# An attention-plus-dense kernel rebuilt: masks as a product, head pairs in one array, the dense stage between attention steps, the max as a relu

## The chip, the cores and the metric

The kernel runs on one core of one Trainium2 chip. The metric is device time in microseconds (us); lower is better. Every comparison runs the kernel before and the other kernel in turn on the same chip. A run counts as slow when it is over 1.5% above the fastest run of the same kernel; comparisons use the fast runs alone. Engines are named as in the profile: PE is the matrix engine (PEld its weight loads), DVE the vector engine, ACT the scalar engine, POOL the general engine, SP the one that issues most transfers.

## The reference, cut to what matters

Two parts follow one another. Attention runs over 4 batches, 8 heads, 768 positions and 64 values a head. A head is either a "retrieval" head (causal mask) or a "streaming" head (causal, and only the first 4 positions or a window of 64). Which it is comes in an input, so it is not known when the kernel is built.

```python
scores = scale * np.matmul(q, k.transpose(0, 1, 3, 2))
causal = rel >= 0                                  # rel = query position - key position
stream_keep = causal & (is_sink | in_win)          # 4 sink positions, window of 64
scores = np.where(mask, scores, -1e9)              # mask: causal, or stream_keep
a = softmax(scores); attn_out = np.matmul(a, v)
```

Its result, 3072 tokens of 512 values, goes through a dense stage with a maximum of two products:

```python
h1 = x @ w1                # 512 -> 1024
h2 = x @ w2                # 512 -> 1024
g = np.maximum(h1, h2)
return g @ w_out           # 1024 -> 512
```

## The kernel before

The kernel before works in three stages, one after the other: masks, attention for all heads, dense for all tokens. It builds two additive masks per head, 768 columns wide, and adds them to the scores **with a matmul** by the identity. Only the 64 rows of one head are live in a score matmul: the query block of one head is padded with zeros, so each head streams over all 128 rows.

```python
for h in range(H):                                   # 16 mask builds of 128x768 on DVE (L95, L99)
    nc.vector.scalar_tensor_tensor(out=msk_g[:, h, :], in0=delta_g, scalar=sf[:, h:h + 1], in1=tri_pad, ...)
    nc.vector.scalar_tensor_tensor(out=msk_0[:, h, :], in0=delta_0, scalar=sf[:, h:h + 1], in1=tri_pad, ...)
# ... (cut: loads, casts on DVE, transposes; psum_sc has bufs=2)
for j in range(NB):                                  # 6 key blocks of one head
    # ... (cut: the loop over pieces of at most 512 columns)
    nc.tensor.matmul(ps[...], lhsT=kt2[:, lo:lo + 128], rhs=qt[...], start=True, stop=False)   # L179 scores
    nc.tensor.matmul(ps[...], lhsT=ident, rhs=dl[:, c0:c0 + cw], start=False, stop=True)       # L184 mask
    nc.scalar.activation(out=at, in_=ps, func=ACT.Exp, scale=scale)                            # L191
    for i in range(j, NB):
        nc.tensor.matmul(po[:, i, :], lhsT=at[:, ...], rhs=vb[:, j, :], ...)                   # L193
for i in range(NB):                                  # six small products per head (L206)
    nc.vector.tensor_scalar_mul(out=x_sb[...], in0=po[:, i, 0:D], scalar1=rez[:, i:i + 1])
# ... (cut: then the dense stage, 6 groups of 512 tokens)
    for fc in range(FC):                             # both products, then the max
        # p1 = w1 block times xt (4 matmuls); g1 = ACT copy of p1
        # p2 = w2 block times xt (4 matmuls)
        nc.vector.tensor_max(out=g[:, fc, :], in0=g1[:, fc, :], in1=p2)
    # out block = sum over fc of g times w_out (8 matmuls each, L251)
```

The softmax here doesn't subtract the row's maximum and nothing guards it: scores larger than these inputs give would overflow.

Of the kernel before, what the change touches and what calls it, by code (L numbers as in the profile page):

```python
# [18 lines left out]
def kernel(  # L19
# [15 lines left out]
    assert D == 64  # L35
    NB = S // 128
    n_sink = int(n_sink)
    window = int(window)
    scale = 1.0 / float(D) ** 0.5
# [5 lines left out]
    n_tok = B * S  # L45
    NT = n_tok // 128
    T4 = 4
    NG = NT // T4
    NTOK = T4 * 128

    consts = ctx.enter_context(tc.tile_pool(name="consts", bufs=1))
    xbuf = ctx.enter_context(tc.tile_pool(name="xbuf", bufs=1))

    ident = consts.tile([128, 128], BF16)
    make_identity(nc, ident)

    tri = consts.tile([128, 128], BF16)
    nc.vector.memset(tri, 0.0)
    nc.gpsimd.affine_select(
        out=tri, in_=tri, compare_op=ALU.is_ge, fill=NEG,  # L60
        base=0, channel_multiplier=-1, pattern=[[1, 128]],
    )

    delta_g = consts.tile([128, S], BF16)
    nc.vector.memset(delta_g, 0.0)
    nc.gpsimd.affine_select(
        out=delta_g, in_=delta_g, compare_op=ALU.is_ge, fill=NEG,
        base=window - 1, channel_multiplier=1, pattern=[[-1, S]],
    )
    delta_0 = consts.tile([128, S], BF16)  # L70
    nc.vector.tensor_copy(out=delta_0, in_=delta_g)
    nc.gpsimd.affine_select(
        out=delta_0, in_=delta_0, compare_op=ALU.is_ge, fill=0.0,
        base=-n_sink, channel_multiplier=1, pattern=[[0, S]],
    )

    ir_handle = _dc.replace(is_retrieval.tensor, dtype=mybir.dt.int32, shape=(2 * H,))
    ir_ap = bass.AP(tensor=ir_handle, offset=0, ap=[[2 * H, 1], [1, 2 * H]])
    ir_raw = consts.tile([1, 2 * H], mybir.dt.int32)
    nc.sync.dma_start(out=ir_raw, in_=ir_ap)  # L80
    sf_1 = consts.tile([1, H], F32)
    nc.vector.tensor_scalar(
        out=sf_1,
        in0=ir_raw.rearrange("o (h two) -> o h two", two=2)[:, :, 0],
        scalar1=-1.0, scalar2=1.0, op0=ALU.mult, op1=ALU.add,
    )
    sf = consts.tile([128, H], F32)
    nc.gpsimd.partition_broadcast(sf, sf_1)  # L88
    tri_pad = consts.tile([128, S], BF16)
    nc.vector.memset(tri_pad, 0.0)  # L90
    nc.vector.tensor_copy(out=tri_pad[:, 0:128], in_=tri)
    msk_g = consts.tile([128, H, S], BF16)
    msk_0 = consts.tile([128, H, S], BF16)
    for h in range(H):
        nc.vector.scalar_tensor_tensor(  # L95
            out=msk_g[:, h, :], in0=delta_g, scalar=sf[:, h:h + 1], in1=tri_pad,
            op0=ALU.mult, op1=ALU.add,
        )
        nc.vector.scalar_tensor_tensor(  # L99
            out=msk_0[:, h, :], in0=delta_0, scalar=sf[:, h:h + 1], in1=tri_pad,  # L100
            op0=ALU.mult, op1=ALU.add,
        )

    w1_sb = consts.tile([128, KC, d_ff], BF16)
    w2_sb = consts.tile([128, KC, d_ff], BF16)
    wo_sb = consts.tile([128, FC, d_model], BF16)
    x_sb = xbuf.tile([128, NT, d_model], BF16)

    with tc.tile_pool(name="qkv", bufs=2) as qkv_pool, \
         tc.tile_pool(name="qt", bufs=2) as qt_pool, \  # L110
         tc.tile_pool(name="awork", bufs=3) as work, \
         tc.tile_pool(name="psum_qkt", bufs=1, space=bass.MemoryType.PSUM) as psum_qkt, \
         tc.tile_pool(name="psum_sc", bufs=2, space=bass.MemoryType.PSUM) as psum_sc, \
         tc.tile_pool(name="psum_o", bufs=2, space=bass.MemoryType.PSUM) as psum_o:
# [180 lines left out]
```

## Time and profile before

| | value |
|---|---|
| median of 3 runs | 320.01 us (318.88 to 321.42) |
| span of the profiled run | 317.9 us |
| masks and start | 0 to 33 us |
| attention | 33 to 181 us, 9.3 us per head pair |
| dense | 181 to 318 us, six groups of 22.7 us |

From the profile's page, the busy time of each engine and the shares of the chain of work that ended last:

```profile
PE 261.1 (82%) x2014; PEld 138.2 (43%) x2048; DVE 150.7 (47%) x409; ACT 151.0 (47%) x289; POOL 34.3 (11%) x74
...
PE 64%; ACT 17%; DVE 9%; issue 7%; DMA 1%; POOL 1%; ACTq 0%; POOLq 0%
```

PE is the engine to relieve, but 82% is an average over three stages. The windows show them. The columns are the stretch, its length, then the busy time of PE, PEld, DVE, ACT and POOL with the number of instructions, the granted clock of PE (1.00 is full speed), the share of the DMA engines and GB/s:

```profile
0.00:33.00 33.00, 14.84 (x107) 7.95 (x109) 22.37 (x33) 8.78 (x15) 7.46 (x20) 1.00 0.70 183
33.00:181.00 148.00, 119.13 (x1276) 70.57 (x1297) 95.72 (x330) 90.43 (x183) 26.80 (x54) 0.97 0.54 131
181.00:318.00 137.00, 127.17 (x634) 59.66 (x643) 32.56 (x48) 51.79 (x91) 0.00 (x0) 1.00 0.12 47
```

In the first 33 us DVE works on masks while PE mostly waits. In attention no engine is full. The dense stage is PE alone (127 of 137 us). The groups of the page say what the attention stage waits for (line, engine, operation, out<-in, count; busy time and mean; idle time before and what ended it):

```profile
L191 ACT ACTIVATE at<-ps 128x768 bf16<-128x768 f32 (+2 forms) x192 | 95.1, 541 | 76.7 <-PE ps L184 71.8
...
L193 PEld LDWEIGHTS <-at 128*128 128x128 bf16 x672 | 33.2, 100 | 60.5 <-ACT at L191 52.5
L184 PE MATMUL ps<-msk_g,ident 128*128 128x512 bf16 (+3 forms) x184 | 52.6, 305 | 2.5 <-DVE msk_g L95 2.4
```

The exp waits 71.8 us for scores and the value matmuls wait 52.5 us for the exp: a round trip with only two score buffers. The mask matmuls (L184) are as many as the score matmuls.

Busy times of single matmuls are modelled ends and overlap, so costs are read from starts in the timeline: 8 matmuls of 512 columns in 1.89 us, and 6 value matmuls of 65 columns in 0.35 us. The last one's own modelled length (0.38 and 0.20 us in the trace) is taken off first: 1.51 us for 7 steps and 0.15 us for 5, so 0.216 and 0.030 us each.

```profile
193.92 1.89 PE L251 MATMUL po_3014<-wo_sb,g 128*128 128x512 bf16 x8
...
104.06 0.35 PE L193 MATMUL po<-vb,at 128*128 128x65 bf16 x6 [0.42 <-ACT at L191]
```

### The profile page before, as it was taken

The numbers are of one execution on the slowest core, as the hardware profiler recorded it, in microseconds if no ns is written. First come the engines' busy times: TensorE is split into PE (matmuls) and PEld (weight loads), VectorE is DVE, ScalarE is ACT, GpSimd is POOL, SyncE is SP. The second block draws the span as 40 slices with busy tenths as digits, with TensorE's granted clock in tenths as the row PEclk, the third lists the DMA queues.
The fourth block names the chain that finished last, engine by engine and source line by source line (L and its number), as shares of the span: only waits on it lengthen the run. The fifth ranks groups of instructions, "written<-read, shape, count | busy, mean of one in ns | idle before, by whom it ended". The sixth has DMA issues, their size and how long they took to land.

```text
span 317.9 us, 5459 instructions
## 1 busy us (share of the span) xinstructions
PE 261.1 (82%) x2014; PEld 138.2 (43%) x2048; DVE 150.7 (47%) x409; ACT 151.0 (47%) x289; POOL 34.3 (11%) x74
## 2 busy tenths in 40 slices
PE   0458479888777888888977799799899899998995
PEld 0224245545344455555543344344444444444442
DVE  2589977766585676567632231141140230330330
ACT  1016336666765766667666432432533534425322
POOL 1142131222132112221200000000000000000000
PEclk9999789999999999999999799999999999999999
DMA  7793276588768566674200001101102102003003
GB/s 177 167 280 137 50 173 157 115 213 255 241 169 183 126 149 141 135 173 101 48 5 2 0 0 66 68 1 66 68 0 97 38 0 99 35 0 132 0 2 132
DMA packets 80844, 31.81 MB, mean 100 GB/s; under 512 B 75698, under 2 KB 75698, under 8 KB 80818
## 3 DMA queue, kind: packets, MB, share of 16 engines
q1 hardware_dynamic: 80818, 31.47, 37.2%
q8 instruction: 16, 0.26, 0.4%
q14 instruction: 10, 0.08, 0.1%
HBM read 25.17 MB, written 6.29 MB: 99 GB/s over the span
## 4 chain that ended last, share of the span: by engine, by line
PE 64%; ACT 17%; DVE 9%; issue 7%; DMA 1%; POOL 1%; ACTq 0%; POOLq 0%
ACT at L191 14%; PE ps L184 9%; PE po L193 8%; PE ps L179 6%; DVE msk_g L95 3%; DVE msk_89 L99 2%; ACT xt L226 2%; DVE x_sb L206 1%; ACT ot L257 1%; DMA out_dram<-ot 1%; PE pxt L222 1%; PE po_3893 L251 1%; PE po_3722 L251 1%; PE po_3551 L251 1%; PE po_3380 L251 1%
## 5 line engine op out<-in xcount | busy, mean ns | idle before, releaser
L191 ACT ACTIVATE at<-ps 128x768 bf16<-128x768 f32 (+2 forms) x192 | 95.1, 541 | 76.7 <-PE ps L184 71.8
L193 PE MATMUL po<-vb,at 128*128 128x65 bf16 x672 | 54.1, 199 | 25.2 <-ACT at L191 17.0
L193 PEld LDWEIGHTS <-at 128*128 128x128 bf16 x672 | 33.2, 100 | 60.5 <-ACT at L191 52.5
L184 PE MATMUL ps<-msk_g,ident 128*128 128x512 bf16 (+3 forms) x184 | 52.6, 305 | 2.5 <-DVE msk_g L95 2.4
L206 DVE TENSOR_SCALAR x_sb<-po,rez 128x64 bf16<-128x64 f32 x192 | 39.5, 275 | 0.1
L184 PEld LDWEIGHTS <-ident 128*128 128x128 bf16 x256 | 25.5, 100 | 11.9 <-issue 3.6
L241 PEld LDWEIGHTS <-w_sb 128*128 128x128 bf16 x192 | 18.9, 98 | 23.8 <-issue 2.1
L251 PEld LDWEIGHTS <-g 128*128 128x128 bf16 x192 | 18.8, 98 | 22.6
L233 PEld LDWEIGHTS <-w_sb 128*128 128x128 bf16 x192 | 18.7, 99 | 20.8 <-issue 0.3
L142 PE MATMUL pqt<-ident,qb 128*128 128x128 bf16 x96 | 15.0, 231 | 10.6 <-POOL ident masks.py:199 10.4
L184 PE MATMUL ps<-msk_89,ident 128*128 128x256 bf16 (+1 forms) x62 | 19.3, 336 | 1.1 <-DVE kt_1525 L145 0.9
L203 DVE RECIPROCAL rez<-po 128x6 f32<-128x6 f32 x32 | 6.1, 194 | 29.0 <-PE po L193 28.4
L143 PE MATMUL pkt<-ident,kb 128*128 128x128 bf16 x96 | 14.3, 232 | 1.8 <-DVE kb L138 1.1
L222 PE MATMUL pxt<-ident,x_sb 128*128 128x128 bf16 x96 | 8.9, 225 | 8.0 <-ACT xt L226 7.5
L226 ACT COPY xt<-pxt 128x512 bf16<-128x512 bf16 x24 | 12.9, 591 | 2.5 <-DVE x_sb L206 2.0
L142 PEld LDWEIGHTS <-qb 128*128 128x128 bf16 x96 | 8.8, 104 | 8.6 <-DVE qb L137 7.5
L143 PEld LDWEIGHTS <-kb 128*128 128x128 bf16 x96 | 8.7, 104 | 6.8 <-issue 4.7
L222 PEld LDWEIGHTS <-x_sb 128*128 128x128 bf16 x96 | 6.9, 100 | 10.6 <-issue 9.3
L165 DVE CAST vb<-vn 128x384 bf16<-128x384 f32 x32 | 11.3, 355 | 0.1
L137 DVE CAST qb<-qn 128x768 bf16<-128x768 f32 x16 | 8.8, 552 | 3.7 <-DMA qn<-in_q_dram 3.6
L138 DVE CAST kb<-kn 128x768 bf16<-128x768 f32 x16 | 8.8, 550 | 0.1
L95 DVE SCALAR_TENSOR_TENSOR msk_g<-delta_g,sf,tri_pad 128x768 bf16<-128x768 bf16 x8 | 8.6, 1074 | 0.2 <-POOL sf L88 0.2
(389 smaller groups left out, 400.9 us busy)
## 6 DMA issues: line engine op xcount, KB each, us to landing
qn<-in_q_dram SPq DMA_DIRECT2D x32, 192.0 KB, 3.5
kn<-in_k_dram SPq DMA_DIRECT2D x32, 192.0 KB, 3.5
vn<-in_v_dram SPq DMA_DIRECT2D x32, 192.0 KB, 2.5
out_dram<-ot SPq DMA_DIRECT2D x24, 256.0 KB, 2.0
wt<-in_moe_w_dram SPq DMA_DIRECT2D x2, 2048.0 KB, 9.4
wt<-in_moe_w_out_dram SPq DMA_DIRECT2D x1, 2048.0 KB, 10.4
ir_raw<-in_is_retrieval_dram SPq DMA_DIRECT2D x1, 0.1 KB
```

Source lines behind the costliest of these rows:

```text
L142: nc.tensor.transpose(pqt[:, n * 128:(n + 1) * 128], qb[:, n], ident)
L143: nc.tensor.transpose(pkt[:, n * 128:(n + 1) * 128], kb[:, n], ident)
L179: nc.tensor.matmul(ps[:, c0:c0 + cw], lhsT=kt2[:, lo:lo + 128], rhs=qt[:, lo + c0: lo + c0 + cw], start=True, stop=False, skip_group_check ...
L184: nc.tensor.matmul(ps[:, c0:c0 + cw], lhsT=ident, rhs=dl[:, c0:c0 + cw], start=False, stop=True, skip_group_check=True,)
L191: nc.scalar.activation(out=at, in_=ps, func=ACT.Exp, scale=scale)
L193: nc.tensor.matmul(po[:, i, :], lhsT=at[:, (i - j) * 128:(i - j + 1) * 128], rhs=vb[:, j, :], start=(j == 0 and i == 0), stop=(j == NB - 1 ...
L206: nc.vector.tensor_scalar_mul(out=x_sb[:, t_idx, h * D:(h + 1) * D], in0=po[:, i, 0:D], scalar1=rez[:, i:i + 1],)
L222: nc.tensor.transpose(pxt[:, tt * 128:(tt + 1) * 128], x_sb[:, gi * T4 + tt, kc * 128:(kc + 1) * 128], ident,)
L226: nc.scalar.copy(out=xt[:, kc, :], in_=pxt)
L233: nc.tensor.matmul(p1, lhsT=w1_sb[:, kc, fc * 128:(fc + 1) * 128], rhs=xt[:, kc, :], start=(kc == 0), stop=(kc == KC - 1),)
L241: nc.tensor.matmul(p2, lhsT=w2_sb[:, kc, fc * 128:(fc + 1) * 128], rhs=xt[:, kc, :], start=(kc == 0), stop=(kc == KC - 1),)
L251: nc.tensor.matmul(po2, lhsT=g[:, fc, tt * 128:(tt + 1) * 128], rhs=wo_sb[:, fc, :], start=(fc == 0), stop=(fc == FC - 1),)
```

## The change

The kernel is rebuilt around four ideas.

1. **Masks multiply the exp.** The mask matmuls go. The blocks on and next to the diagonal ("near") are multiplied by a 0/1 mask on DVE after the exp; blocks further off get a per-row bias of -30000 in the exp for streaming heads, and no product.
2. **Head pairs share the array.** The two heads of a pair lie in rows 0 to 63 and 64 to 127; each score matmul uses 64 rows, so two can run at once.
3. **The max as a relu.** max(h1, h2) = relu(h1 - h2) + h2, so max(xW1, xW2) Wo = relu(x(W1-W2)) Wo + x(W2 Wo). The kernel computes W1-W2 (POOL) and the merged W2 Wo (W2 cast, transposed, then multiplied by Wo) once, at run time. This is the **weight preparation**.
4. **The dense stage of batch b is laid between the attention steps of batch b+1.** The work of a list called `fill` is spread over the steps. In batch 0, which has no earlier dense work, the list holds the weight preparation.

The diff is nearly the whole file; its core:

```diff
-        nc.vector.scalar_tensor_tensor(out=msk_g[:, h, :], ...)      # additive, 16 of 128x768
+        for m in range(3):                                           # 0/1, 24 of 128x256 (L122)
+            nc.vector.scalar_tensor_tensor(out=msk[:, h, m, :], in0=(far0 if m == 0 else far),
+                scalar=nsf[:, h:h + 1], in1=causal, op0=ALU.mult, op1=ALU.add)
...
-    nc.tensor.matmul(ps[...], lhsT=ident, rhs=dl[:, c0:c0 + cw], start=False, stop=True)
+    for (j, q0, w, off) in segs:
+        for hh in range(2):
+            nc.tensor.matmul(sc[hh][:, off:off + w],
+                lhsT=kt[64 * hh:64 * hh + 64, j * 128:(j + 1) * 128],
+                rhs=qt[64 * hh:64 * hh + 64, q0:q0 + w], start=True, stop=True)          # L209
+    nc.scalar.activation(out=at[:, 0:n], in_=sc[hh][:, 0:n], func=ACT.Exp, scale=scale, bias=bias)
+    if kind == "near":
+        nc.vector.tensor_mul(out=at[:, 0:n], in0=at[:, 0:n], in1=mk)                      # L222
...
+def prep_w2(c):                                                      # L138, x4
+    nc.vector.tensor_copy(out=w2_bf[:, c, :], in_=wts["w2"][:, c, :])
+def prep_wo(c):                                                      # L141, x4
+    nc.vector.tensor_copy(out=wo_bf[:, 2 * c:2 * c + 2, :], in_=wts["wo"][:, 2 * c:2 * c + 2, :])
+def prep_wd(c):                                                      # L144, x4
+    nc.gpsimd.tensor_sub(out=wd_bf[:, c, :], in0=wts["w1"][:, c, :], in1=wts["w2"][:, c, :])
+def w2_transpose(f): ...   # 4 transposes (L150) and a DVE copy (L151), x8
+def w_merge(c): ...        # 8 matmuls of 512 columns (L156) and a DVE cast (L158), x4
...
-    nc.vector.tensor_max(out=g[:, fc, :], in0=g1[:, fc, :], in1=p2)
+    nc.vector.tensor_relu(out=gts[g][:, f, :], in_=ps[:, 0:GT])      # one product less per block
...
+    fill = []
+    for c in range(KC):
+        fill += [(512, lambda c=c: prep_w2(c)), (512, lambda c=c: prep_wo(c)), (512, lambda c=c: prep_wd(c))]
+    fill += [(512, lambda f=f: w2_transpose(f)) for f in range(FC)]
+    fill += [(FC * 512, lambda c=c: w_merge(c)) for c in range(KC)]
+    ...
+        if hp == 0 and b > 0:
+            fill = fill + dense_steps(b - 1)
```

The score buffers go from two to four; casts of q, k and v move from DVE to POOL; the copy of the transposed k goes to ACT, that of q stays on DVE. The transposes of q, k, x and W2, the merge and the dense products share two PSUM buffers (`ps_mm`; PSUM is where the kernel has PE write its results).

## The prediction

> **What bounds it now.** Three stages follow one another.
>
> 1. Start. The timeline shows DVE building sixteen masks (0.93 to 1.07 us each) until about 33 us. The table of windows gives PE 4.5 us busy in the first 20.
> 2. Attention, about 33 to 181 us, some 9.3 us per head pair. No engine is full: per 40 us PE is busy 32 to 33 (modelled), ACT 25 to 26, DVE 19 to 27. In the groups the exp waits 71.8 us for scores, and the AV weight loads wait 52.5 us for the exp: a score-exp-AV round trip with two score buffers.
> 3. Dense, about 181 to 318 us: six groups of 22.7 us each (distance of the same output tile in the chain of waits). PE-bound: 38.2 of 40 us busy.
>
> **Unit costs on PE from the timeline** (starts, not modelled ends): 512-column matmul 0.216 us (8 in 1.89); 128-column transpose 0.055 us; AV matmul (65 columns) 0.030 us (6 in 0.35).
>
> **PE work before, estimated from these:** dense 288 x 0.216 x 2 = 124 us; scores 36 us; mask matmuls 36 us; AV 20 us; transposes 16 us. About 232 us.
>
> **After:**
> - Mask matmuls (36 us of PE) go. In their place are six bf16 DVE products per pair, about 0.35 us each, and a bias in the far exps.
> - Scores: 37 us if the heads run one after the other, 18 if the two 64-row halves run together. The Trainium skill (TensorEngine Tiling, Key Properties) says that tiles run independently, but that a change of tiling mode drains the array. This kernel changes mode about twelve times a pair; at an estimated 0.1 us each that is 19 us, so packing roughly pays for its drains. No trace before shows either.
> - Dense: max(h1,h2) Wo = relu(x(W1-W2)) Wo + x(W2 Wo). Up halves, down grows by half: 246k columns against 295k, 104 us. The merge adds 9 us once.
> - AV and transposes stay, 37 us.
> - Sum: 168 us, about 187 with drains.
>
> ACT keeps its exps (same columns, 104 us) and gets kt copies, loses the g1 copies and xt copies. DVE per pair: masks 2, qt copy 0.9, norm 1.4 (one wide multiply instead of six of 0.275 us per head), xt 0.5, relu 1.9: 7 us. POOL takes the casts, about 3 us a pair. None exceeds PE's time per pair.
>
> **Critical path after.** Start: 24 small masks at about 0.35 us plus chains of tiny DVE operations let the first scores through at about 15 us, instead of 33. Batch 0, which has no dense work yet: four pairs at about 8 us (ACT, latency, merge), until about 47. Then twelve pairs mixed with dense: attention 3.5, drains 1.2, dense 6.5, plus about 5% stalls: 11.9 us each, 143 us. The last batch's dense stage stands alone: 26 us of matmul, pacing by the two shared PSUM buffers, the last transpose and the last output, 34 us. Sum 224 us.
>
> **Prediction: 224 us, 204 to 248.** Faster by over 2%: 0.97; within 2%: 0.02; slower: 0.01.
>
> **Right or wrong is shown by:** first scores near 15 us; paired score matmuls with starts a few ns apart and a gap at each switch; PE over 85% busy from 50 us on; twelve pairs of 11 to 12.5 us; a tail of 30 to 36 us with PE only; no mask matmuls; DVE near 130 us busy, ACT near 120.
>
> **What would make it wrong:** weights that land late, so that an in-order DVE or POOL stalls at their casts (batch 0 then ends at 60 us or later); POOL casts several times slower than 1 us, slowed by DVE; the two dense PSUM buffers held by a DVE that waits for exp; drains of 0.2 us or more; or better, drains near zero, and a total near 205.

## The result, and the profile after

| | before | after |
|---|---|---|
| median | 319.44 us (4 runs) | 255.34 us (254.75 to 256.27, 4 runs) |
| ratio of fast runs | | 0.7989, 95% interval 0.7953 to 0.8026 |
| span of the profiled run | 317.9 us | 252.9 us |

A ratio here is the mean time of one kernel's fast runs over that of the other's fast runs of the same rounds, so it is not quite the ratio of the medians. The change is 20% faster, but 31 us slower than predicted, and outside the range of 204 to 248. A repeat later (e13_after) gave 255.52 us.

The page of the kernel after, the same two lines as before:

```profile
PE 212.4 (84%) x1869; PEld 111.9 (44%) x1888; DVE 150.1 (59%) x323; ACT 127.7 (50%) x233; POOL 54.9 (22%) x72
...
PE 67%; DVE 22%; ACT 5%; issue 3%; DMA 2%; ACTq 0%
```

PE gave up 49 us. DVE has as much work as before, and its share of the chain of waits rose from 9% to 22%. Where, the windows tell; the columns are as above:

```profile
0.00:21.80 21.80, 2.46 (x18) 1.78 (x19) 19.43 (x49) 2.30 (x2) 8.63 (x15) 1.00 1.02 223
21.80:37.60 15.80, 15.04 (x128) 7.76 (x127) 7.44 (x18) 13.39 (x25) 1.75 (x3) 1.00 1.01 384
37.60:58.40 20.80, 10.40 (x59) 6.19 (x60) 15.93 (x22) 1.03 (x1) 14.61 (x8) 1.00 1.19 263
58.40:79.90 21.50, 19.27 (x209) 10.34 (x211) 14.75 (x30) 16.34 (x32) 5.14 (x8) 1.00 0.28 65
79.90:221.40 141.50, 137.94 (x1326) 72.68 (x1338) 83.14 (x190) 90.92 (x169) 24.76 (x38) 1.00 0.30 86
221.40:253.00 31.60, 27.27 (x134) 13.12 (x135) 9.43 (x17) 3.72 (x7) 0.00 (x0) 1.00 0.16 59
```

Set against the prediction, stage by stage:

| stage | predicted | measured | difference |
|---|---|---|---|
| start, until the first scores | 15 | 21.8 | +6.8 |
| batch 0, pairs 1 and 2 | 16 | 15.8 | -0.2 |
| batch 0, a hole between pairs 2 and 3 | 0 | 20.8 | +20.8 |
| batch 0, pairs 3 and 4 | 16 | 21.5 | +5.5 |
| twelve pairs mixed with dense work | 143 | 141.5 | -1.5 |
| tail | 34 | 31.6 | -2.4 |
| sum | 224 | 253.0 | +29.0 |

The remaining 2 us lie between the span and the device time (252.9 against 254.75 in the profiled run), which the sum had left out.

So the stage that the rebuild is about came out as predicted, and the miss sits in the first 80 us. The hole is the largest piece. In the third window ACT, the engine that does the exps, is busy 1.03 of 20.8 us: its only instruction is a copy, in front of which it sat 17.5 us idle. This is the timeline of ACT (start, length, instruction, and in brackets the idle time before it and what ended that):

```profile
37.10 0.47 ACT L218 ACTIVATE at<-sc,bias_j 128x256 bf16<-128x256 f32 x1 [0.19 <-PE sc L209]
55.12 1.03 ACT L188 COPY kt<-tp 128x768 bf16<-128x768 bf16 x1 [17.54 <-PE tp L181]
59.07 1.08 ACT L218 ACTIVATE at<-sc 128x512 bf16<-128x512 f32 x2 [2.92 <-PE sc L209]
```

The chain of waits through the hole (start, length, what held it; pieces of under 0.3 us left out):

```profile
38.16 5.17 DVE w_bf L138 x4
43.33 0.47 DVE x L275
43.79 0.67 DVE w2t L151 x2
...
45.31 0.81 PE xtp L284 x6
46.14 0.57 DVE xt L286
...
47.80 5.17 DVE wo_bf L141 x4
52.97 0.33 DVE w2t L151
53.31 0.93 DVE qt L186
...
54.28 0.80 PE tp L181 x6
...
55.73 2.77 PE wmp L156 x6
58.49 0.97 PE sc L209 x6
```

All of it is weight preparation (w_bf, w2t, wo_bf, wmp), or pair 3 coming up piece by piece between it. PE and POOL at the same time, from the timeline:

```profile
43.38 0.39 PE L150 MATMUL w2tp<-ident,w_bf 128*128 128x128 bf16 x2 [2.34 <-DVE w_bf L138]
...
47.85 0.80 PE L181 MATMUL tp<-ident,qb 128*128 128x128 bf16 x6
53.36 0.59 PE L150 MATMUL w2tp<-ident,w_bf 128*128 128x128 bf16 x4 [4.71 <-DVE w2t L151]
...
40.04 10.56 POOL L144 TENSOR_TENSOR wd_bf<-w_186,w_182 128x1024 bf16<-128x1024 f32 x4
```

The q transposes of pair 3 stood behind the transposes of W2 and began only at 47.85. They were done by 48.65, but the copy that takes them out of PSUM (qt, L186) began at 53.2, behind the four casts of Wo. Only then could the k transposes and the scores follow. Meanwhile both of the shared PSUM buffers were full, one with the q transposes and one with a block of W2, so PE stood still until 53.36. No run changed the number of these buffers; what more of them would give is untested.

No cast waited for its weights. Page part 6 gives the median time from issue to landing:

```profile
w_182<-in_moe_w_dram SPq DMA_DIRECT2D x1, 2048.0 KB, 10.3
wo<-in_moe_w_out_dram SPq DMA_DIRECT2D x1, 2048.0 KB, 14.0
w_186<-in_moe_w_dram SPq DMA_DIRECT2D x1, 2048.0 KB, 19.1
```

In the trace these were issued at 17.5, 20.0 and 20.8 us, so W2 was there at 27.8, Wo at 34.0 and W1 at 39.9 us. The casts of W2 began at 38.1 and those of Wo at 47.7, 10 and 14 us later. Only the POOL subtraction began right after its weight had landed, at 40.04. Whether an earlier arrival would have changed the order in which the casts were placed is another question (e11).

The casts themselves are longer than such a cast need be. The groups with shapes kept apart give a mean of 1374 ns:

```profile
L141 DVE CAST wo_bf<-wo 128x1024 bf16<-128x1024 f32 x4 | 5.3, 1374 | 0.0
L138 DVE CAST w_bf<-w_182 128x1024 bf16<-128x1024 f32 x4 | 5.3, 1374 | 0.0
```

Single ones took 0.65 to 0.71 us or 1.3 us, and two took 2.8 us, about as long as one POOL subtraction (2.3 to 2.8 us) that ran at the same time. Each of the four long casts ended 0.55 us after the end of the POOL instruction that was running when it began: they were held until POOL was done. The start shows the same on a smaller scale. This is the timeline of DVE and of POOL while the masks are built:

```profile
6.29 0.48 DVE L122 SCALAR_TENSOR_TENSOR msk<-far_135,nsf,causal 128x256 bf16<-128x256 f32 x1
6.68 1.05 DVE L122 SCALAR_TENSOR_TENSOR msk<-far,nsf,causal 128x256 bf16<-128x256 f32 x1
...
6.37 1.08 POOL L169 CAST qb<-qn 128x768 bf16<-128x768 f32 x1 [5.48 <-DMA qn<-in_q_dram]
```

A mask build takes 0.47 to 0.48 us alone (starts 0.396 apart) and 1.04 to 1.11 us beside a POOL cast. That happened to 8 of the 24. They run from 5.89 to 20.10 us: 24 x 0.396 = 9.5 us, and 4.7 us for the eight. All eight ended 0.28 us after the POOL cast beside them.

The rest of the plan held. In the mixed stage PE is busy 137.9 of 141.5 us. The two score matmuls of a pair start 3 to 4 ns apart in 136 of 160 cases. At 200 changes between 64-row and 128-row matmuls, the median gap beyond streaming was 0.098 us going in and 0.096 us coming out.

### The profile page after: what moved, and what is told of

The parts are those of the page before. It is cut to its first block, busy times and chain, and to the rows that moved or that the text cites. A ratio compares the mean times of both kernels' runs of the same rounds, so it can differ in the third digit from the quotient of the medians.

```text
span 252.9 us, 4818 instructions
## 1 busy us (share of the span) xinstructions
PE 212.4 (84%) x1869; PEld 111.9 (44%) x1888; DVE 150.1 (59%) x323; ACT 127.7 (50%) x233; POOL 54.9 (22%) x72
## 4 chain that ended last, share of the span: by engine, by line
PE 67%; DVE 22%; ACT 5%; issue 3%; DMA 2%; ACTq 0%
PE h L306 17%; PE y L320 15%; PE po L232 11%; PE sc L209 9%; DVE msk L122 5%; PE y L317 5%; DVE at L222 4%; PE tp L181 4%; PE wmp L156 3%; DVE x L275 3%; ACT at L218 3%; PE xtp L284 3%; DVE wo_bf L141 2%; DVE w_bf L138 2%; DMA ir_raw<-in_is_retrieval_dram 2%
## 5 line engine op out<-in xcount | busy, mean ns | idle before, releaser
L218 ACT ACTIVATE at<-sc 128x512 bf16<-128x512 f32 (+1 forms) x96 | 48.9, 565 | 24.7 <-PE sc L209 24.5
L222 DVE TENSOR_TENSOR at<-at,msk 128x512 bf16<-128x512 bf16 (+1 forms) x96 | 39.5, 426 | 21.7 <-ACT at L218 21.2
L209 PE MATMUL sc<-qt,kt 64*128 64x256 bf16 (+3 forms) x320 | 42.2, 300 | 10.8 <-DVE qt L186 9.4
L306 PE MATMUL h<-xt,wd_bf 128*128 128x384 bf16 x256 | 50.8, 326 | 0.5 <-ACT ot L323 0.3
L320 PE MATMUL y<-wo_bf,gt 128*128 128x512 bf16 x190 | 47.7, 379 | 0.1
L309 DVE TENSOR_SCALAR gt<-h 128x384 bf16<-128x384 f32 x64 | 35.1, 554 | 20.0 <-PE h L306 18.6
L218 ACT ACTIVATE at<-sc,bias_j 128x512 bf16<-128x512 f32 (+1 forms) x64 | 34.2, 588 | 10.7 <-PE sc L209 10.6
L306 PEld LDWEIGHTS <-wd_bf 128*128 128x128 bf16 x256 | 22.7, 97 | 15.5 <-issue 3.3
L317 PE MATMUL y<-wm_bf,xt 128*128 128x512 bf16 x82 | 24.8, 380 | 0.7
L169 POOL CAST kb<-kn 128x768 bf16<-128x768 f32 x16 | 14.2, 888 | 35.5 <-PE tp L181 30.7
L218 ACT ACTIVATE at<-sc,bias_94 128x512 bf16<-128x512 f32 x32 | 20.3, 693 | 0.1
L186 DVE COPY qt<-tp 128x768 bf16<-128x768 bf16 x16 | 16.2, 1018 | 3.3 <-PE tp L181 2.9
## 6 DMA issues: line engine op xcount, KB each, us to landing
w_182<-in_moe_w_dram SPq DMA_DIRECT2D x1, 2048.0 KB, 10.3
```

Of the source, the lines that this page charges most:

```text
L169: nc.gpsimd.tensor_copy(out=t.rearrange("p n h d -> p h n d"), in_=src.rearrange("p h m (r d) -> p h (m r) d", d=D))
L186: nc.vector.tensor_copy(out=o, in_=i)
L209: nc.tensor.matmul(sc[hh][:, off:off + w], lhsT=kt[64 * hh:64 * hh + 64, j * 128:(j + 1) * 128], rhs=qt[64 * hh:64 * hh + 64, q0:q0 + w], ...
L218: nc.scalar.activation(out=at[:, 0:n], in_=sc[hh][:, 0:n], func=ACT.Exp, scale=scale, bias=bias)
L222: nc.vector.tensor_mul(out=at[:, 0:n], in0=at[:, 0:n], in1=mk)
L306: nc.tensor.matmul(ps[:, 0:GT], lhsT=wd_bf[:, c, f * 128:(f + 1) * 128], rhs=xts[b][:, c, g * GT:(g + 1) * GT], start=(c == 0), stop=(c == ...
```

## The experiments

Theories for the lost 30 us: **queue order** (long pieces of preparation stand in the in-order queues of DVE, POOL and PE in front of the small steps that the next pair needs), **contention** (POOL work stretches DVE work), and **the work itself** (the preparation, the masks and the mode switches cost what they cost). The expectations may use letters of their own for these, and may count pairs from 0 where the text here counts from 1. "First dense" is the start of the first dense matmul, 79.9 us in the kernel after; the "longest gap" is between the starts of two neighbouring exps, 22.0 us there. The batches ran on different chips (numbers 6, 5, 9, 5 and 5), so the ratio to the kernel before, taken on the same chip, is the safer comparison between them. For e1 to e4 the verdict against the kernel before is "unclear": its own runs spread from 315.21 to 322.63 us there, three of seven of them slow. Their ratios are quoted with their intervals.

### First batch: contention, order, lateness, masks

**e1_nosub**, without the POOL subtraction; the result is wrong.

```diff
-        nc.gpsimd.tensor_sub(out=wd_bf[:, c, :], in0=wts["w1"][:, c, :], in1=wts["w2"][:, c, :])
+        nc.gpsimd.memset(wd_bf[:, c, :], 0.03)
```

> POOL's weight subtraction is replaced by a memset of wd (wrong result on purpose); the order on DVE stays. In the kernel after the change nothing is scored between 37 and 58 us, and the eight weight casts on DVE take 10.5 us there, 0.65 us the shortest and 2.8 us the longest. Theory A (contention: DVE's casts are stretched by POOL's subtraction, and that makes the hole): casts 0.65 us each, 5.2 us in all, and most of the hole gone (under 8 us left); total under 240 us. Theory B (order: the next pair's transposes and scores stand behind the whole weight preparation in the queues of DVE and PE): casts become short as well, but the hole keeps at least 12 us; total 247 to 252 us. Theory C (weights land too late): no change, within 1 us of 255.

Measured: 251.75 us, ratio 0.7933 (0.7857 to 0.8008); first dense 77.1, longest gap 17.7. Six of the eight casts took 0.65 to 0.69 us, two 1.3 to 1.4. So contention is real, but with it gone the hole is only about 4 us shorter. The total gained 2 us by the ratio and 4 by the medians, and the intervals overlap, so it is not clear of the noise. Nor is the run quite clean: the memsets wait for no weight and ran at 0.8 to 4.4 us, and the first scores came at 23.3 us instead of 21.8. Queue order is favoured.

**e2_castact**, the eight weight casts on ACT.

```diff
-        nc.vector.tensor_copy(out=w2_bf[:, c, :], in_=wts["w2"][:, c, :])
+        nc.scalar.copy(out=w2_bf[:, c, :], in_=wts["w2"][:, c, :])
```
(and the same for Wo)

> The eight weight casts move from DVE to ACT, which sits idle for 17 us of the hole; result correct. A: no DVE cast meets POOL's subtraction, the hole falls under 10 us, total about 243. B: the transposes of the weights and the merge still stand ahead of the next pair; the hole shrinks by the casts (up to 10 us) but the next scores wait for the merge all the same: total 245 to 250. C: no change, since the weights land when they did (the last one at about 40 us).

Measured: 249.58 us, ratio 0.7855 (0.780 to 0.7911); first dense 73.2, longest gap 14.7. Ten microseconds of DVE casts taken off the queue in front of the copies shorten the hole by 7.

**e3_late**, the preparation one pair later: casts and subtraction in pair 2, transposes and merge from pair 3.

```diff
+        if i == 1:
+            fill = fill + prep
+        if i == 2:
+            fill = fill + merge
-        left = HP - hp
+        left = 1 if i == 1 else HP - hp
```

> The weight preparation starts one pair later: casts and subtraction among pair 1's steps, transposes and merge among pairs 2 and 3. Nothing is made cheaper. B: pair 2's scores no longer wait for the merge, the longest stretch without an exp in the first 80 us falls from 20 us to under 8, batch 0 ends near 68 us instead of 80, total about 243 (240 to 247). A: the casts still meet the subtraction, so at least half of the gain fails to come: total 249 to 255. C: the weights have landed by then in any case, no statement.

Measured: 250.11 us, ratio 0.7872 (0.7812 to 0.7931); first dense 73.3; gaps of 11.4 us at 46.4 and 6.0 us at 61.2. This is in the range written down for contention (249 to 255), not in that for order (240 to 247), although the casts were no longer stretched (0.69 us each). The hole splits into two. Later, the subtractions met the mask products, which take 0.41 us alone; here are two of them in the timeline of DVE:

```profile
58.42 4.47 DVE L222 TENSOR_TENSOR at<-at,msk 128x512 bf16<-128x512 bf16 x2 [0.26 <-ACT at L218]
```

**e4_masks**, only the masks of the first pair before the first scores, the others two heads at a time in pairs 1 to 3.

```diff
+        def make(h):
             for m in range(3):
                 nc.vector.scalar_tensor_tensor(out=msk[:, h, m, :], ...)
+        make(0)
+        make(1)
...
+            if b == 0 and hp + 1 < HP and si in (4, 7):
+                make_masks[0](2 * hp + (2 if si == 4 else 3))
```

> Only the two heads of the first pair get their masks before the first transposes; the other eighteen masks are traced between later steps. Theory M (the masks are a plain delay at the start): first scores near 12 us instead of 21.8, total 9 us less (246). B or C: the first two pairs run earlier, but the next wait, for weights that land at 28 to 40 us, stays where it is; total within 3 us of 255.

Measured: 249.58 us (one of four runs slow), ratio 0.7886 (0.7791 to 0.7981). First scores at 10.4 us instead of 21.8; first dense 71.6; the gap of 21.3 us is still there, at 29.0. Of 11 us at the start, 8 came through to the first dense matmul and some 6 to the end, which is between the two expectations.

### Second batch: contention alone, a later merge, packing

**e5_dvesub**, the subtraction on DVE; correct results.

```diff
-        nc.gpsimd.tensor_sub(out=wd_bf[:, c, :], ...)
+        nc.vector.tensor_sub(out=wd_bf[:, c, :], ...)
```

> The weight subtraction moves from POOL to DVE (about 1.2 us for each of four, estimated from the mask builds: 0.47 us for 256 columns); result correct. Contention: no DVE instruction above 1.3 us any more, where the shipped change has casts of 2.8 us. The casts save 5 us, the subtraction costs DVE 5: if only that mattered, no gain (254 to 256). Order (B): the hole stays above 14 us, since the scores of pair 2 still stand behind the merge; total 250 to 254, as in the run with POOL's subtraction taken out (251.8).

Measured: 255.74 us, ratio 0.8017 (0.7976 to 0.8058); first dense 80.2; gaps of 17.6 and 8.3 us. No gain. What contention cost is paid back as DVE time in the same queue. It is not a clean comparison, though: the value matmuls start 54 ns apart until some time after 60 us here, and 32 ns apart from about 60 on in the kernel after, so PE was longer at half pace (more of this in the fifth batch).

**e6_later**, casts and subtraction meant for pairs 2 and 3, transposes of W2 and merge in pair 4.

```diff
+        if i == 1:
+            fill = fill + prep
+        if i == 3:
+            fill = fill + merge
-        left = HP - hp
+        left = 2 if i == 1 else HP - hp
```

> Casts and subtraction are traced among pairs 1 and 2, all transposes of weights and the merge among pair 3, so that no pair's own transposes wait behind them for one of the two shared PSUM buffers. Nothing is cheaper. B (order and the shared buffers): pairs 2 and 3 start about 9 us after their predecessors, no stretch of over 6 us without an exp before the last of batch 0, the first dense matmul comes at or before 66 us instead of 79.9, total 238 to 242 (the rest takes 174 us from there in every kernel so far). A (contention is what matters): POOL's subtraction now meets mask products, the gain stays under 5 us, as in the kernel that prepared one pair later (250).

Measured: 252.47 us (one slow run), ratio 0.7894 (0.7818 to 0.797). The edit does not quite do what was meant: `left` is 2 again in pair 3, so a quarter of the casts and subtractions is left for pair 4. The exps of pairs 3 and 4 now start at 40.2 and 50.4 us, but a gap of 17.6 us opens behind pair 4 instead, and the first dense matmul comes at 78.1. The expected 238 to 242 us were missed: the hole moved with the work. The last W2 cast, on which each of the eight transposed blocks of W2 depends, came only at 56.7 us and took 2.8. Contention again met the mask products, as DVE and POOL in the timeline show:

```profile
51.69 7.32 POOL L144 TENSOR_TENSOR wd_bf<-w,w 128x1024 bf16<-128x1024 f32 x3
52.44 4.36 DVE L222 TENSOR_TENSOR at<-at,msk 128x512 bf16<-128x512 bf16 x2
```

Here too the value matmuls stay 54 ns apart until nearly 70 us, so PE did the moved work at half pace. For these two reasons the run says little about order by itself.

**e7_unpacked**, scores over all 128 rows with zero-padded q, as in the kernel before: no shared array, no mode switches (output buffers 3 to 2, for space).

```diff
-                    lhsT=kt[64 * hh:64 * hh + 64, j * 128:(j + 1) * 128],
-                    rhs=qt[64 * hh:64 * hh + 64, q0:q0 + w],
+                    lhsT=kt[:, j * 128:(j + 1) * 128],
+                    rhs=qt[hh][:, q0:q0 + w],
```

> The heads of a pair no longer share the array: each head's scores use all 128 rows against queries padded with zeros (made once), so there is no change of tiling mode. Counted from the trace of the change: 200 switches at a median of 0.096 us go (19 us), the second halves stream separately (18 us more on PE). DVE gets one more copy of 0.6 to 1 us per pair. If the switches cost what the gaps say: total 253 to 258, the same within 2%. If packing is worth its stream time and switches are hidden: about 270. If switches cost more than their gaps: under 248.

Measured: 258.68 us, ratio 0.8114 (0.8064 to 0.8165), against 0.801 (0.7976 to 0.8044) for the change. The mixed stage is 146.2 us instead of 141.5:

```profile
79.00:225.20 146.20, 138.88 (x1341) 85.12 (x1339) 94.10 (x201) 91.00 (x169) 23.75 (x38) 1.00 0.29 83
```

So packing, net of its 200 drains, is worth about 3 us in all (1.3%), and that is an upper bound: this kernel also has 11 us more DVE work there (94.1 against 83.1), because q is copied in two halves. "Packing roughly pays for its drains" was right.

**e8_grouped**, two score steps at a time, to halve the mode switches.

```diff
-        for i in range(n):
-            seq.append(av(i))
-            if i + 2 < n:
-                seq.append(sc(i + 2))
+        for i in range(2, n, 2):
+            seq += [sc(i), sc(i + 1), av(i - 2), av(i - 1)]
+        seq += [av(n - 2), av(n - 1)]
...
-            spend(quota)
+            if si not in (0, 2, 6):
+                spend(quota * 12 / 9)
```

> Score steps are issued two at a time, so that 64-row work comes in three groups per pair instead of six: switches fall from about 200 to 110. If each costs 0.096 us on the bottleneck: 7 to 9 us less, total 246 to 248. If the exps of a group then come too late for PE, stalls before the value matmuls eat it: 253 to 258.

Measured: 262.82 us, ratio 0.8222 (0.8165 to 0.8279), slower. The switches were 192, not the expected 110 or so: the order of instructions in the built program was not the order of the source. Only 103 of the packed halves remained, of 136. This is a miss of the experiment; it says nothing about fewer switches.

### Third batch: how much is there to win, and combinations

**e9_noprep**, no preparation at all (constants in its place); wrong.

```diff
-        nc.vector.tensor_copy(out=w2_bf[:, c, :], in_=wts["w2"][:, c, :])
+        nc.gpsimd.memset(w2_bf[:, c, 0:8], 0.03)
...
-    fill += [(512, lambda f=f: w2_transpose(f)) for f in range(FC)]
-    fill += [(FC * 512, lambda c=c: w_merge(c)) for c in range(KC)]
+    fill += [(512, lambda c=c: nc.gpsimd.memset(wm_bf[:, c, :], 0.03)) for c in range(KC)]
```
(and the same for Wo and W1-W2)

> The whole weight preparation is taken out of the change (casts, subtraction, transposes, merge; the tiles are filled with a constant on POOL, wrong result on purpose). It bounds what the preparation costs, however its parts hide one another. If it is the cause of the late batch 0: four pairs of about 8.5 us from 22 us on, the first dense matmul near 57 us instead of 79.9, total 230 to 234. If something else holds batch 0 back (transposes, exps, loads of the pairs): first dense matmul after 68 us, total over 242.

Measured: fast runs of 236.35 and 238.26 us, two slow ones of 241.82 and 243.04; no ratio. First dense 60.8, no gap over 3.8 us. From first scores to first dense it takes 36.1 us (24.7 to 60.8), against 58.1 in the kernel after: the preparation costs 22 us of batch 0, and about 18 us of the total (255.4 on another chip against a mean of 237.3 for its fast runs). That is between the expected 230 to 234 and the 242 that would have named another cause. It also shows that batch 0 without the preparation is 9.0 us a pair, not 8.

**e10_both**, e5 and e6 together (edits as there, with the same quarter left for pair 4).

> Both single steps together: subtraction on DVE (alone: 255.7) and preparation later (alone: 252.5). If contention and order hide one another, the two together give clearly more than the sum of the single gains (0 and 3 us): total 240 to 246. If neither is the cause: 251 to 254.

Measured: fast runs of 249.91, 251.37 and 253.45 us, one slow run of 305.8 us at a granted clock of 0.689, from which nothing is read; ratio 0.7858 (0.7791 to 0.7925). The expected 240 to 246 was missed; contention and order had not merely been hiding each other.

**e11_ileave**, one weight matrix loaded after each of the loads of pairs 2, 3 and 4, instead of all three after pair 4.

```diff
         if i == 0:
             constants()
-    load_weights()
+        else:
+            load_weights(("w2", "wo", "w1")[i - 1])
```
(cut: the lines by which `load_weights` loads only the matrix named)

> Only the order of the loads changes: one weight matrix after each of the pairs 1, 2 and 3 instead of all three behind the four pairs, so W2 lands near 20 us instead of 28. C (weights late, on the chip and in the static order that was built around their expected arrival): the gap without exps falls under 12 us, total 242 to 248. A and B: the merge and the subtraction still stand in the way, total 250 to 255.

Measured: 248.53 us, ratio 0.7759 (0.7719 to 0.780); first dense 72.6; gaps of 8.3 and 5.0 us. The casts of W2 start at 24.8 us instead of 38.1. This is more than the kernel's own trace had made me expect, as no cast there waited for a transfer. Loading earlier also changes where the scheduler of the framework places the casts, so this run can't tell the arrival from the order. What it does say is that the hole shrinks when the long pieces are spread.

**e12_all**, masks as in e4, loads as in e11, subtraction on DVE, and the preparation in three stages (casts, then transposes and subtraction, then merge, one per pair), still in large pieces.

```diff
+    stages = {1: [prep_w2(c) ...] + [prep_wo(c) ...],
+              2: [w2_transpose(f) ...] + [prep_wd(c) ...],
+              3: [w_merge(c) ...]}
...
+        fill = fill + stages.pop(i, [])
-        left = HP - hp
+        left = 1 if b == 0 else HP - hp
```
(lambdas shortened)

> Masks just in time, weights loaded between the pairs, subtraction on DVE, casts among pair 1's steps, transposes of weights among pair 2's, merge among pair 3's. If the three causes (masks at the start, contention, order) add up to the missing time: first scores at 10 to 11 us, no gap without exps over 6 us, first dense matmul at 50 to 54 us, total 224 to 229. If a further cause is missing: over 236.

Measured: 244.44 us, ratio 0.7635 (0.759 to 0.768); first dense 67.4; gaps of 8.0 and 8.1 us. Better, but not the expected 224 to 229. The gaps had names, in the timeline of DVE:

```profile
42.93 3.79 DVE L149 CAST wo_bf<-wo 128x1024 bf16<-128x1024 f32 x4
46.65 1.00 DVE L194 COPY qt<-tp 128x768 bf16<-128x768 bf16 x1
...
56.35 4.62 DVE L152 TENSOR_TENSOR wd_bf<-w,w 128x1024 bf16<-128x1024 f32 x4
60.89 0.69 DVE L166 CAST wm_bf<-wmp 128x512 bf16<-128x512 f32 x1
61.49 1.01 DVE L194 COPY qt<-tp 128x768 bf16<-128x768 bf16 x1
```

Both times the q copy of the next pair starts right behind four large pieces that had come out of the scheduler as one run (and, the second time, one copy more). Its transposes were done at 44.1 and 59.1 us, so it stood ready for about 2.5 us each time. The spreading in the source does not spread them in the queue; smaller pieces might.

### Fourth batch: small pieces

**e13_after**, the change itself again, as a control.

> Control: the change as it is, on the chip of the other three. 254 to 257 us, first dense matmul at 79 to 81 us, gap without exps 20 to 23 us.

Measured: 255.52 us, ratio 0.801 (0.7976 to 0.8044); first dense 79.9, longest gap 21.2.

**e14_fine**, as e12, but in pieces of one block, and with the stages cut elsewhere: W2 is cast 128 columns at a time right before their transposes, Wo row block by row block, and W1-W2 is taken 128 columns at a time on DVE, six of the eight blocks only right before the dense step that needs them.

```diff
-    def prep_w2(c): ...
+    def prep_wo(f):
+        nc.vector.tensor_copy(out=wo_bf[:, f, :], in_=wts["wo"][:, f, :])
+    def prep_wd(f):
+        cols = slice(f * 128, (f + 1) * 128)
+        nc.vector.tensor_sub(out=wd_bf[:, :, cols], in0=wts["w1"][:, :, cols], in1=wts["w2"][:, :, cols])
     def w2_transpose(f):
+        cols = slice(f * 128, (f + 1) * 128)
+        nc.vector.tensor_copy(out=w2_bf[:, :, cols], in_=wts["w2"][:, :, cols])
...
+            for f in range(FC):
+                if b == 0 and g == 0 and f + 2 < FC:
+                    steps.append((0, lambda f=f: prep_wd(f + 2)))
+                steps.append((4 * GT, up(g, f)))
...
+    stages = {1: [w2_transpose(f) ...], 2: [prep_wo(f) ...], 3: [w_merge(c) ...] + [prep_wd(f) for f in range(2)]}
```
(masks and loads as in e4 and e11; lambdas shortened)

> Masks just in time, weights loaded between the pairs, and the preparation cut up: W2 is cast one block of 128 columns at a time just before that block is transposed, Wo row by row, the subtraction on DVE block by block, six of the eight blocks just before the dense step that needs them; merge among pair 3's steps. If long instructions in front of short ones on the in-order queues made the gap: no gap without exps over 5 us, first dense matmul at 52 to 58 us, total 228 to 234 (the large pieces gave 244.4 and gaps of 8 us). If the work as such is what costs: 239 to 245.

Measured: **239.39 us** (239.0 to 240.35), ratio 0.7514 (0.748 to 0.7547). It beats both kernels: 25% under the one before, 6% under the change, with correct results. First scores 11.9, first dense 63.8, gaps of 6.4 and 6.3 us. The expected 228 to 234 was missed; the time fell into the range written down for "the work as such" (239 to 245), so the preparation also costs something as work. The windows (start, batch 0, mixed stage, tail):

```profile
0.00:11.90 11.90, 1.66 (x14) 1.23 (x16) 8.81 (x31) 2.31 (x2) 4.33 (x10) 1.00 0.80 189
11.90:63.80 51.90, 44.01 (x391) 24.28 (x391) 45.75 (x101) 29.96 (x55) 15.54 (x20) 0.93 1.10 288
63.80:205.60 141.80, 139.05 (x1350) 72.63 (x1350) 84.01 (x192) 92.30 (x171) 24.83 (x38) 1.00 0.33 90
205.60:237.00 31.40, 27.37 (x136) 13.11 (x135) 9.48 (x17) 3.77 (x7) 0.00 (x0) 1.00 0.16 59
```

In batch 0 DVE is now busy 45.75 of 51.9 us, 88%.

**e15_fine_merge_late**, as e14 with the merge behind the first dense steps, in pairs 5 and 6.

```diff
-              3: merges + [prep_wd(f) for f in range(2)]}
+              3: [prep_wd(f) for f in range(2)]}
...
+            if b == 0 and g == 0:
+                steps += merges
```

> As e14, but the merge (32 matmuls of 512 columns, 7 us at full clock) comes after the first eight dense steps of batch 0, among pair 4's and 5's steps. If merging in batch 0 costs nothing there because PE has room: 4 to 7 us slower than e14. If the merge in batch 0 stands in front of scores, at half clock: as fast as e14 or faster.

Measured: 246.42 us, ratio 0.773 (0.7695 to 0.7765), 7 us slower than e14, though its first dense matmul comes earlier, at 61.5. The merge belongs into batch 0, where PE has room, and not into the stage where PE is the limit.

**e16_fine_only**, the small pieces and their stages (as in e14) alone; masks and loads as in the change.

> Only the cutting up of the preparation, with masks and loads as in the change. In-order queues with long pieces: 242 to 247, against 255.3 for the change, with the gap under 10 us. The work as such, or weights late: 250 to 255.

Measured: 245.58 us, ratio 0.7702 (0.7666 to 0.7737), which is 10 us faster than the change, as expected (242 to 247). First dense 69.8, longest gap 9.9. The window of batch 0:

```profile
21.70:69.80 48.10, 43.05 (x383) 24.61 (x382) 36.20 (x81) 28.94 (x53) 10.19 (x15) 1.00 0.97 272
```

The work is the same as in e5, only cut up and laid differently: DVE is busy 36.2 us in batch 0 here and 37.9 in e5. (Six of the eight subtractions stand behind the start of the dense stage in the source; in the trace only two began after it.) So the length of the pieces in front of the small copies, with their place, is worth 10 us.

### Fifth batch: what still holds batch 0

In these traces the value matmuls start 54 ns apart in the early part of batch 0 and 32 ns apart later. In the kernel after, the step comes at about 60 us; in e14 at about 32 us, with a fall back from 36 to 43 us. Transposes (107 ns against 55) and matmuls of 512 columns (427 against 216) show the same, so PE works at half pace there, although the granted clock of the page reads 1.00. Whether this or the full DVE makes batch 0 long was the last question.

**e17_warm**, e14 plus dummy matmuls on zeros while PE waits for its first operands.

```diff
+    def warm_up(n):
+        warm = ps_sc.tile([128, 512], F32, tag="sc", name="warm")
+        for _ in range(n):
+            nc.tensor.matmul(warm, lhsT=zero[:, 0:128], rhs=zero, start=True, stop=True)
+    warm_up(20)                 # before the first transposes
...
+    warm_up(8)                  # before the first scores
```
(one argument cut; `zero` is a tile of zeros)

> The best version so far (masks as needed, interleaved weight loads, preparation in one-block pieces) plus 20 dummy 512-column matmuls on zeros while PE has nothing to do before the first transposes, and 8 more between these and the first scores. In that version's trace the value matmuls start 54 ns apart until about 30 us and 32 ns apart later, though the granted clock of the records is 1.00. Theory W (this half pace of PE is what holds batch 0 up): value matmuls 30 to 35 ns apart from the first scores on, first dense matmul at 56 to 60 us instead of 63.8, total 231 to 236 us. Rival R (batch 0 of this version is bound by DVE, busy 45.8 of its 51.9 us): the pace goes up, but the first dense matmul stays at 62 to 65 us and the total at 238 to 241 us. If the pace does not change at all, neither is tested.

Measured: 238.37 us (237.61 to 239.71, 6 runs), ratio 0.7482 (0.745 to 0.7515), no different from e14; first dense 62.5. The dummies did get up to pace: they start 427 ns apart until 5.1 us and 216 ns apart from then on. But PE had nothing to do from 10.7 to 13.3 us, and little after that, and fell back: from about 16 to 43 us the value matmuls are 54 ns apart again, but for some 3 us from 32 us on. The pace did not change where it mattered, so by its own terms this run tests neither theory.

**e18_keepwarm**, one more dummy of 256 columns in front of each score step of batch 0.

```diff
+        if b == 0:
+            nc.tensor.matmul(sc[0][:, 0:256], lhsT=zero[:, 0:128], rhs=zero[:, 0:256], start=True, stop=True)
```

> As e17_warm, and in batch 0 one more dummy matmul of 256 columns in front of each score step (24 in all, 2.6 to 5 us of PE), so that PE does not fall back in the pauses of batch 0. W: if PE falls back in e17_warm and not here, the first dense matmul comes at 54 to 60 us and the total is 1 to 4 us under e17_warm. R: no gain over e17_warm, or 0 to 3 us lost, because the dummies stand in front of the scores while DVE sets the pace.

Measured: 241.78 us (241.45 to 242.23), ratio 0.7583 (0.7561 to 0.7605), 3.4 us slower than e17. The value matmuls still start 54 ns apart until about 36 us and again at about 44, and the first dense matmul comes at 66.6. The few dummies did not keep PE up. They cost their time, but not only that: the scheduler also placed the q transposes of pair 2 in front of the first scores, which came at 14.8 us. Whether PE's pace or DVE's work is what makes the 52 us of batch 0 stays open.

One thing e17 did show is how the clock column is to be read. Here is the same stretch in e14 and then in e17, in both of which value matmuls start 54 ns apart for most of the time:

```profile
11.90:40.00 28.10, 24.55 (x198) 13.41 (x198) 23.57 (x56) 16.69 (x31) 7.41 (x10) 0.93 1.05 320
```

```profile
11.90:40.00 28.10, 22.63 (x203) 13.45 (x203) 24.73 (x58) 16.95 (x31) 7.64 (x10) 0.62 1.08 329
```

In e17 the column reads 1.00 from the start (also while the first dummies start 427 ns apart), then 0.50 from about 16 us on, and 0.62 over this stretch. In e14 it reads 1.00 until about 36 us, with the value matmuls at half pace for most of that. So the column seems to show 1.00 until a first fall is recorded, and its mean can't be compared between these runs. The spacing of equal matmuls is the safer reading.

### All runs at a glance

| run | median us | ratio of fast runs | first scores | first dense | longest gap |
|---|---|---|---|---|---|
| after | 255.34 | 0.7989 | 21.8 | 79.9 | 22.0 |
| e1_nosub (wrong) | 251.75 | 0.7933 | 23.3 | 77.1 | 17.7 |
| e2_castact | 249.58 | 0.7855 | 22.0 | 73.2 | 14.7 |
| e3_late | 250.11 | 0.7872 | 21.4 | 73.3 | 11.4 |
| e4_masks | 249.58 | 0.7886 | 10.4 | 71.6 | 21.3 |
| e5_dvesub | 255.74 | 0.8017 | 22.0 | 80.2 | 17.6 |
| e6_later | 252.47 | 0.7894 | 22.0 | 78.1 | 17.6 |
| e7_unpacked | 258.68 | 0.8114 | 22.4 | 79.0 | 22.4 |
| e8_grouped | 262.82 | 0.8222 | 22.1 | 81.9 | 20.8 |
| e9_noprep (wrong) | 240.04 | none | 24.7 | 60.8 | 3.8 |
| e10_both | 252.41 | 0.7858 | (profile of a slow run) | | |
| e11_ileave | 248.53 | 0.7759 | 20.3 | 72.6 | 8.3 |
| e12_all | 244.44 | 0.7635 | 11.6 | 67.4 | 8.1 |
| e13_after | 255.52 | 0.8010 | 22.0 | 79.9 | 21.2 |
| **e14_fine** | **239.39** | **0.7514** | 11.9 | 63.8 | 6.4 |
| e15_fine_merge_late | 246.42 | 0.7730 | 10.3 | 61.5 | 7.1 |
| e16_fine_only | 245.58 | 0.7702 | 21.7 | 69.8 | 9.9 |
| e17_warm | 238.37 | 0.7482 | 13.7 | 62.5 | 7.8 |
| e18_keepwarm | 241.78 | 0.7583 | 14.8 | 66.6 | 6.6 |

The medians are over all runs; those of e4, e6, e9 and e10 have slow ones among them.

## Why the prediction was right or wrong, point by point

**Right: the stages that it worked out from counted work.** Twelve mixed pairs took 141.5 us (143 predicted; 11.8 a pair against 11.9), the tail 31.6 (34). The unit costs from starts held in the trace from about 60 us on (216 ns for 512 columns, 55 to 56 ns for a transpose, 30 to 35 ns for a value matmul); before that they were near double. So that pairs 1 and 2 took 15.8 us, where 16 was predicted, is partly luck: the 8 us a pair had full pace and a share of the merge in them. The drains held too: the Trainium skill (TensorEngine Tiling (Array Packing), Key Properties) says that a change of tiling mode drains the array but gives no figure; the guess of 0.1 us each met a measured 0.096 to 0.098 us. And packing about pays for its drains (e7: at most 1.3%). That the two halves run together agrees with the Trainium skill (TensorE: Matmul & The Clock Gate, Part 3: Packing small matmuls), which gives starts about 4 ns apart; this trace has 3 to 4 ns.

**Wrong, first: "let the first scores through at about 15 us".** It was 21.8. The mechanism was right, the size of a term was off: 24 mask builds at an estimated 0.35 us are 8.4 us; measured, they take 14.2 us, at 0.396 us each plus 0.6 us for each of the eight that met a POOL cast. Small operations behind them made up the rest. That the casts had been moved to POOL was counted as free for DVE. It was not: DVE was held by POOL. e4 shows that most of this start can be had back by building only the masks that are needed.

**Wrong, mainly: "Batch 0 ... four pairs at about 8 us (ACT, latency, merge), until about 47".** It ended at 79.9. The merge was put down as "9 us once" on PE, and the other parts of the preparation (12 wide casts and subtractions, 12 copies out of PSUM, 32 transposes) were put down nowhere. "None exceeds PE's time per pair" was the check, and it adds up each engine by itself. What failed is the overlap: pieces on engines with room were taken to cost nothing, but an engine with room is no protection when the next pair's small step stands behind a long one in its queue. What the runs showed in its place:

- The preparation costs 22 us of batch 0 and about 18 us of the total (e9).
- About 10 us of it is the length and place of the pieces (e16). Four casts in a row are 5.2 us in which a copy of 1.0 us, on which PE and ACT hang, waits. This was shown twice: in the kernel after, where the q transposes were done at 48.65 and their copy began at 53.2, and in e12, where two copies stood ready for about 2.5 us behind long runs.
- About 4 us of the hole is contention of POOL and DVE (e1; 2 to 4 us of the total, not clear of noise), but it can't be had by moving the subtraction to DVE in large pieces (e5).
- Moving the large pieces to other pairs moves the hole (e6; there with some pieces later than meant and PE longer at half pace). Spreading them over earlier arrivals (e11) helps by 7 us, with order and arrival not told apart.
- The gains overlap: e14 has all of them and gains 16 us, with a batch 0 that still takes 51.9 us where 36.1 would do without preparation. There DVE is busy 88% of the time, and PE runs at half pace for part of it. e17 and e18 tried to take the half pace away and did not manage to; which of the two sets the time there is open. How much of the 22 us in the kernel after is the half pace is open as well: six of its merge matmuls stood in front of the scores at 427 ns each, not 216.

**The listed doubts.** "Weights that land late, so that an in-order DVE or POOL stalls at their casts (batch 0 then ends at 60 us or later)" foresaw the stall and the figure, but for the wrong reason: W2 and Wo had landed 10 and 14 us before their casts began (e11 leaves open whether their place in the queue hung on the arrival). "POOL casts several times slower than 1 us" did not happen (0.82 to 1.36 us), it was DVE that slowed. DVE's busy time came to 150 us, not 130; 57.6 of it fell in the first 80 us, with 10.6 us of weight casts that had not been counted. ACT's came to 128, not 120.

## What to carry to other kernels

When work is laid between the steps of a pipeline, count for each piece not only its engine time but what stands behind it in that engine's queue: a piece of several microseconds in front of a one-microsecond copy delays everything that hangs on the copy, on engines that look idle. Cut preparation into pieces of the size of the steps that it is laid between (here 16 us, with the masks and loads spread as well), and put only as much of it up front as the first step needs. Before the first run, look at the stretch in which the pipeline fills: a stage predicted to about 1% doesn't help when the first quarter of the time was put down as "about 8 us a pair".

## What the Trainium skill lacked or had wrong

- GPSIMD Engine Reference, section 8, Key points: it says that POOL shares its SBUF interfaces with VectorE, with contention for DVE instructions with two SBUF inputs or in a 2-port mode, and gives no size in that section. (The skill as a whole is not silent on it, so this is no gap, only numbers.) A DVE cast of 128x1024 went from 0.65 us to as much as 2.8 us and two mask products from 0.8 us to 4.4 us, each held until the POOL subtraction (2.3 to 2.8 us) beside it was done; a mask build went from 0.47 to 1.05 us beside a POOL cast of 0.8 to 1.1 us. Its statement that DVE is about twice as fast elementwise agrees: a subtraction of 128x1024 took 2.3 to 2.8 us on POOL and 1.16 us on DVE (e12, 4.62 us for four).
- TensorEngine Tiling (Array Packing), Key Properties: it has no figure for the drain of a mode change. Here it is 0.096 to 0.098 us of PE for each switch (200 switches).
- TensorE: Matmul & The Clock Gate, Part 1: its cold and warm spacings (426.7 and 215.7 ns at 512 columns) agree with e17 (427 and 216 ns, the change 3.8 us after the first matmul). It does not say how busy PE must be to get out of the cold state. Here PE streamed at half pace for about 0.7 to 0.8 of the time from 22 to 37.6 us (columns counted at 512 in 427 ns, packed pairs once) and stayed at half pace; in e17 the fall came after a pause of 2.6 us and loose work behind it.
- No page that I read says that the clock shown by a profile can stand at 1.00 while matmuls start at half pace. Here the value matmuls of batch 0 start 54 ns apart, against 32 later, in windows that read 1.00 (21.8 to 37.6 us in the kernel after). The same Part 1 does warn that such records are unreliable.
